# One block of filter rows first, the key weights in two halves, and a new written order

## The chip, the cores and the metric

The kernel runs on one core of a Trainium2 chip. The core has a matrix engine (TensorE, in the profile PE, with its weight loads as PEld), a vector engine (VectorE, DVE), an engine for functions (ScalarE, ACT), a general engine (GpSimd, POOL), and a queue engine that only issues transfers here (SyncE, SP). Sixteen DMA engines move the data. All times are device microseconds of one execution; the time of a kernel is the median of its runs.

## The reference

Two computations that share no data, both over 2048 positions and 576 channels in bf16, whose results stand beside each other in the output.

```python
# A: a long convolution with gates
k_shift = sum over t < 4 of shift(k, t) * shift_k[:, t]      # short filter over positions
kv = k_shift * v
y  = irfft(rfft(pad(kv)) * rfft(pad(ssm_k)))[:2048] + kv * ssm_D
a  = q * y

# B: linear attention, 32 heads of 18 channels
q, k, v = split(x @ wqkv)
phi(t) = (t + 1 if t > 0 else exp(t)) + 1e-6
kv  = phi(k).T @ v                 # per head, over all positions
z   = sum of phi(k) over positions
o   = (phi(q) @ kv) / (phi(q) . z + 1e-6)
b   = o @ wo

out = concat(a, b)
```

## The kernel before

The program builds a list of 838 operations (`P.op`, `load`), each with the buffers that it reads and writes. Their order, and for each the engine that runs it, is written out in the string `PLAN`: `P` is TensorE, `A` ScalarE, `D` VectorE, `G` POOL and `S` an issue on SP, followed by the operation's number. `PLACES` gives the address or PSUM bank of every buffer. `_issue` reads both; nothing is decided at run time. Every engine runs its operations strictly in that order and waits at each one until its operands are there and until the buffer that lay at the same address before has been used up. One more rule ties POOL to VectorE: a product or sum of POOL (marked `two`) waits for the last such product of VectorE that stands ahead of it in the order. SP issues its loads in order too, and no more than eight transfers are under way at a time.

Part A does the convolution as matrix products. The filter `ssm_k` comes in five blocks of up to 128 rows (`hs`); TensorE turns each (`htr`, L437), ScalarE or VectorE copies it to `hT` (`hev`), and POOL or VectorE adds `ssm_D` to its first tap (`hD`). For each of three groups of 192 channels follow a first transform (`s1h`, L468, eight products of four matmuls, each evicted to `Ch`), three transposes on VectorE (`trh`, L507), and a second small transform (`s2h`, L516, twelve groups of four matmuls on quarters of the array, evicted to `sph`). The data side is the same (`s1u`, `Cu`, `tru`, `s2u`, `spu`) after the short filter: VectorE multiplies the keys by the taps (`tap`, L402), the halves are summed (`tap+`) and multiplied by v (`tapv`), on VectorE or POOL; for two of the six pieces a DMA that POOL issues adds the first halves (`acc`, L408). Then two products of spectra (`p1`, `p2`, L236), an inverse transform in two stages (`i1`, L552, evicted to `V`; `i2`, L577, evicted to `yb`), the product with q (`yq`, or directly from PSUM as `i2q`) and the store (`yo`).

Part B turns the first 512 rows of x on TensorE (`xtr`, L323; its copies are `xev`, the copy of the last columns is `x4c`); the other rows come by a transposing DMA. For each of 16 blocks of 128 positions `kproj` makes the key product (`k`, L624: ten matmuls, two halves of 288 columns by five blocks of 128 rows of the weights `wk`), ScalarE its exponential (`kexp`) and VectorE phi (`kphi`). `qproj` (L645) does the same for q. `G` (L674) sums phi(k) with x over all positions; `kv` and `M` (L709, L771) fold the value and output weights into one matrix, `msev` (L802) scales its last rows; `den` and `rden` give 1 over the denominator, which goes to memory (`rw`) and comes back spread over rows (`rr`), and `pqn` multiplies phi(q) by it, on VectorE or POOL. `out` (L814) makes the output product, `oev` its copy and `oo` its store.

Ahead of everything TensorE runs nine matmuls on a constant (`fill`, L845). In the order before, SP issues first the two halves of x's first rows, the table with the identity (`idw`), the key weights (`wqktk`, then `wqkk` in one transfer, L355 and L357), `Drow`, then filter blocks 0 and 1 and one half of the transform's table, filter block 2, the other half, and the shift taps (`srow`). TensorE's order is: fill, the four steps of x, k1, k0, filter block 0, k2, filter block 1, then `s1h` of the first group.

Of the kernel before, what the change touches and what calls it, by code (L numbers as in the profile page):

```python
# [183 lines left out]
def kernel(  # L184
# [430 lines left out]
    def kproj(r):  # L615
# [2 lines left out]
        xT = xTg[r // 4]  # L618
        st = "k%d" % r

        def mm(e):
            for hh in range(2):
                for t in range(5):
                    nc.tensor.matmul(ps.t[:, hh, 0:HALF],  # L624
                                     lhsT=cols(xT.t[0:KT[t], t, :], r),
                                     rhs=wk.t[0:KT[t], t, HALF * hh:HALF * hh + HALF],
                                     start=(t == 0), stop=(t == 4))
        P.op("P", mm, rd=[wk] + ([xT] if r // 4 in XD else [(xT, (r % 4 // 2, t0)) for t0 in (0, 4)]), wr=[ps], name="k", mm=[(288, 128, 128)] * 10, st=st)
        P.op("A", lambda e: nc.scalar.activation(  # L629
            out=eb.t[:], in_=ps.t[:, :, 0:HALF], func=ACTF.Exp, bias=neg1.t[:]), rd=[ps, neg1], wr=[eb], name="kexp",  # L630
             n=576, st=st)
# [240 lines left out]
P98 S423 D35 S19 P95 P368 G0 D37 A15 A99 A369 S18 S41 P366 D100 G228 D367 P101 P375 A96 S472 D97 P372 A102 A377  # L872
A374 D376 P394 G4 D373 S59 D370 A395 P386 P392 D103 G10 G14 P384 P426 D387 A393 P424 G12 S56 G378 D385 A23 D427
P388 A425 P433 D379 G42 A434 P435 P382 S55 G428 D389 D436 P390 P380 P437 D391 A383 P443 D438 A381 P429 D405 P475
P441 A444 P431 D414 S24 S40 S58 P473 A430 A442 D396 P439 A432 A440 S60 P146 P417 A147 P415 S25 A474 G477 D476 D445
A418 P104 D148 A105 P143 S46 P401 P397 A416 P446 P448 S51 D106 P452 A144 P155 A449 A453 A398 D454 A402 P149 P152
A156 A150 D145 A447 S478 P408 D463 G47 D157 A153 P403 P399 P457 D151 A409 D400 S50 S45 P468 P170 A458 A404 P406
D469 P410 P461 D154 A462 D65 P459 P421 P161 A171 A411 P158 S48 A460 P412 S43 P466 P455 G52 D172 P419 D64 A407 A422
P164 D75 A456 P481 D74 D66 P470 A413 A467 P464 S230 P450 A420 P167 A165 G67 A451 A471 A162 D163 P479 A465 A480 A168
P197 D166 P200 A482 P191 A159 A192 D169 A201 D160 A198 D202 D193 P110 P185 D76 A111 G44 G483 D112 D199 P173 S594  # L880
A186 P134 P176 A174 G49 S61 D175 D187 A135 P122 A177 P179 G77 D178 D136 P107 S652 P119 A123 D124 A180 A108 P137 D78
D85 S229 A120 P188 D109 D181 A138 S595 D121 G68 S232 A189 P140 P128 S38 A141 D139 D190 P125 D84 A129 D142 P131 D130
P486 D86 P116 A126 A487 A132 A117 D127 P113 G87 S231 A114 S62 A39 S653 D133 D118 P194 P494 P182 D115 A183 P223 D88
A224 P484 A485 A195 D70 D79 A495 P226 A225 S17 P208 D69 D80 A227 S63 P236 D237 D238 P203 G71 D184 P239 D196 P243
P488 G81 D204 A209 A205 A210 P492 D240 D241 S552 D244 P498 A489 P206 D242 D245 A493 P490 A499 D72 D73 A491 P496
S553 S246 P218 A497 S247 A207 D219 P537 D220 A538 P531 S259 P529 A530 P221 P533 D82 S260 S258 P527 A532 A222 S254
D83 A534 P535 D89 A536 S261 P213 A528 P618 S265 P620 P608 P211 D90 A621 P610 A609 P606 D255 A212 D619 D266 A611
P614 D214 S269 G91 G270 P216 A607 D500 S252 P503 A215 P507 G262 A615 D518 P519 D509 P612 D217 A504 D508 P616 A520
D92 S263 S674 P541 P233 A613 P539 A617 A542 S271 A540 D93 P699 D235 P281 G272 D234 S267 P693 D700 P275 D694 A282
P273 P279 A276 A274 P277 D280 S248 A278 P691 A692 P685 P695 P283 D622 A696 S256 D686 P687 D284 S673 P629 P516 G253  # L890
A688 P627 P514 D517 P697 G264 D564 A630 P689 G268 A698 P332 A333 P347 A628 P355 A690 D664 G249 P357 P350 A356 A515
A351 P667 P669 D348 P671 A358 D585 S250 D701 A672 S631 P521 P512 G251 P505 P330 P352 A670 P327 P325 A513 A331 A668
D522 D353 A328 P665 D506 S573 P510 S574 D743 S22 P706 A326 P625 S329 P525 A666 P501 A511 P623 D643 A624 G257 P300
P345 S359 A707 P340 A626 P342 A341 A526 P302 P750 P704 P748 D502 P648 S354 G675 S632 A346 D301 P590 A343 D722 P650
G676 D705 D591 P362 S711 A649 D363 P360 P312 P567 A303 D651 A749 P565 A751 S731 P644 A361 S732 P523 D313 P646 A568
P744 S349 P708 A524 P315 D543 S753 D316 P310 P337 P317 D647 P569 A745 D311 S334 P586 D634 P725 A566 A645 S304 D655
P571 P723 A709 A338 P727 S364 A318 A728 P290 A726 S344 A587 P320 P683 A321 P307 A570 S319 A572 S314 D724 P729 P746
D291 A684 P702 P550 P548 D654 A703 P677 A747 P305 P660 P681 A306 A308 A661 D633 P641 S752 A682 P292 A551 P658 A293
A549 A659 P335 A642 D576 P679 A680 P297 A678 P635 D730 P546 P592 P544 D754 D755 D733 A336 S710 P588 D734 D713 A636
A593 A589 P756 P637 D712 A545 P295 A638 P639 A640 D298 P656 P737 A657 P739 A740 P662 A547 A738 A663 P741 P718 P720  # L900
P758 A721 P760 A759 P762 D757 P800 A801 A761 P735 D575 D555 S294 S94 P794 D296 A795 P796 D597 P802 D763 S339 A742
P577 D719 A803 A797 A736 D596 P806 S309 P716 P788 P714 A717 D554 P579 D804 A807 D798 P322 P808 A715 P824 P826 P790
S299 A323 D825 P832 A789 A791 P600 S324 P560 A809 A601 S799 A827 P581 A833 P812 P562 D792 P598 A599 D578 P814 D582
A561 D815 P830 A580 G810 G828 A563 S793 D813 P583 A584 D831 D816 S805 P558 P820 D821 G834 D559 P602 P556 S811 P818
P604 P285 D819 D603 A557 S829 S835 A605 D822 S817 D286 S823 P287 A288 S289 P784 P782 D785 A783 D786 P776 S787 A777
P778 A779 P772 D773 D780 S781 P764 P770 P766 D767 A771 D774 S775 A765 D768 S769
"""
PLACES = """
# [16 lines left out]
"""  # L925


# [28 lines left out]
```

## Time and profile before

| | us |
|---|---|
| median of 3 runs | 160.5 (160.44 to 160.75) |
| the profiled execution's own time | 161.04 |
| its span, first to last instruction | 159.2 |
| TensorE busy | 150.4 (94%) |
| VectorE busy | 143.3 (90%) |
| ScalarE busy | 122.7 (77%) |
| POOL busy | 63.2 (40%) |

The profile has one profiled execution. Its page gives busy time by engine, the span in 40 slices, the DMA queues, the chain of work that ended last, and the costliest groups of instructions. A group's line gives the source line, the engine, the operation, what it writes and reads, how often, its busy time, the mean duration of one in ns, the idle time of the engine ahead of it, and what ended that idle time. The view of windows gives the busy time by stage, the timeline the instructions in order of time, and the view of waits who waited for whom. A line L236, L231 or L229 is a helper's (products and sums, copies on VectorE, copies on ScalarE), so these are told apart by the names of what they write.

### The profile page before, as it was taken

What the parts mean: (1) busy time and instruction counts of PE and PEld (TensorE: products, weight loads), DVE (VectorE), ACT (ScalarE), POOL (GpSimd) and SP (SyncE); (2) the same over time, 40 slices, a digit from 0 to 9 for tenths busy, and PEclk for the clock granted to TensorE, in tenths of its full rate; (3) what the DMA queues carried; (4) which work ended last, traced back from release to release, by engine and by line L of the source; (5) the groups of instructions that cost most, each with busy time, mean ns of one, the idle gap of its engine ahead of it and who ended that gap; (6) DMA issues with size and microseconds to landing.
All of it is one profiled execution on the core that took longest, in us unless ns stands there. A gap on an engine that the chain in (4) does not pass through costs nothing.

```text
span 159.2 us, 4176 instructions
## 1 busy us (share of the span) xinstructions
PE 150.4 (94%) x1663; PEld 119.5 (75%) x1663; DVE 143.3 (90%) x183; ACT 122.7 (77%) x224; POOL 63.2 (40%) x51
## 2 busy tenths in 40 slices
PE   6897899999999999999999999999999999999970
PEld 2686785545677889787888878787777889999960
DVE  1537999999999999899899999999999999998981
ACT  3148799999996566561869599899989999896860
POOL 8901100110199170606920594996891000004400
PEclk9999999999999999999999999999999999999997
DMA  5999699999999128496925597891647449415575
GB/s 164 301 401 291 155 218 377 214 200 277 397 371 302 31 36 296 197 252 213 164 81 183 155 161 234 268 368 67 245 171 252 174 120 408 178 43 161 151 211 148
DMA packets 26317, 34.37 MB, mean 216 GB/s; under 512 B 15802, under 2 KB 20923, under 8 KB 25530
## 3 DMA queue, kind: packets, MB, share of 16 engines
q1 hardware_dynamic: 25754, 32.54, 65.8%
q0 software_dynamic: 544, 1.57, 5.6%
q8 instruction: 13, 0.21, 0.5%
q14 instruction: 6, 0.05, 0.1%
HBM read 20.86 MB, written 4.99 MB: 162 GB/s over the span
## 4 chain that ended last, share of the span: by engine, by line
PE 82%; DVE 5%; DMA 3%; ACT 3%; issue 2%; SPq 1%; DVEq 1%; ACTq 0%
PE ps_all L645 13%; PE ps_all L814 13%; PE ps_all L624 12%; PE ps_all L674 12%; PE ps_all L552 10%; PE ps_all L468 9%; PE ps_all L516 5%; PE ps_all L577 4%; DMA wk<-in_B_wqkv_dram 3%; DVE Cu L231 2%; PE ps_all L437 2%; SPq L222 1%; ACT sph L229 1%; PE ps_all L709 1%; DVE q L236 1%
## 5 line engine op out<-in xcount | busy, mean ns | idle before, releaser
L645 PE MATMUL ps_all<-xT,wq 128*126 128x512 bf16 (+1 forms) x100 | 24.0, 381 | 0.1
L814 PE MATMUL ps_all<-M,pqT 126*128 126x288 bf16 (+1 forms) x160 | 22.1, 287 | 0.0
L236 POOL TENSOR_TENSOR m<-m 128x1536 bf16<-128x1536 bf16 (+1 forms) x4 | 15.5, 3885 | 15.4 <-DVE m L236 15.4
L624 PE MATMUL ps_all<-wk,xT 128*128 128x288 bf16 x160 | 21.1, 286 | 0.5 <-DMA wk<-in_B_wqkv_dram 0.5
L402 DVE TENSOR_TENSOR m<-kh,Wj 128x3072 bf16<-128x3072 bf16 x12 | 20.5, 1752 | 0.1
L624 PEld LDWEIGHTS <-xT 128*128 128x128 bf16 x160 | 17.4, 109 | 3.6 <-issue 0.8
L814 PEld LDWEIGHTS <-pqT 126*128 126x128 bf16 (+1 forms) x160 | 16.8, 110 | 3.8 <-issue 2.0
L468 PEld LDWEIGHTS <-Gsb 128*128 128x128 bf16 x192 | 16.1, 98 | 4.2 <-issue 2.2
L645 PEld LDWEIGHTS <-wq 128*126 128x126 bf16 (+1 forms) x100 | 12.6, 131 | 7.9 <-issue 1.7
L552 PE MATMUL ps_all<-Esb,sph 128*128 128x128 bf16 x144 | 18.0, 219 | 0.0
L552 PE MATMUL ps_all<-Esb,X 128*128 128x128 bf16 x144 | 17.9, 219 | 0.0
L236 POOL TENSOR_TENSOR pqT<-pqT,rb 126x1024 bf16<-126x1024 bf16 (+1 forms) x8 | 16.8, 2138 | 2.5 <-DMA rb<-r_scr 2.1
L229 ACT ACTIVATE spu<-ps_all 128x512 bf16<-128x512 f32 x30 | 17.0, 636 | 0.6 <-PE ps_all L516 0.6
L229 ACT ACTIVATE Cu<-ps_all 128x768 bf16<-128x768 f32 x20 | 15.7, 853 | 2.0 <-PE ps_all L468 2.0
L229 ACT ACTIVATE V<-ps_all 128x512 bf16<-128x512 f32 x29 | 16.4, 661 | 1.2 <-PE ps_all L552 1.2
L674 PE MATMUL ps_all<-pk,x_sb 128*128 128x289 bf16 (+1 forms) x128 | 17.1, 287 | 0.0
L629 ACT ACTIVATE ek<-ps_all,neg 128x576 bf16<-128x576 f32 x16 | 11.7, 740 | 6.5 <-PE ps_all L624 6.4
L229 ACT ACTIVATE Ch<-ps_all 128x768 bf16<-128x768 f32 x18 | 14.2, 855 | 3.1 <-PE ps_all L468 3.1
L229 ACT ACTIVATE sph<-ps_all 128x512 bf16<-128x512 f32 x29 | 16.1, 625 | 0.3 <-PE ps_all L516 0.3
L648 ACT ACTIVATE eq<-ps_all,neg 126x512 bf16<-126x512 f32 (+1 forms) x20 | 13.7, 708 | 2.9 <-PE ps_all L645 2.6
L552 PEld LDWEIGHTS <-sph 128*128 128x128 bf16 x144 | 14.1, 98 | 0.7 <-issue 0.5
L674 PEld LDWEIGHTS <-x_sb 128*128 128x128 bf16 x128 | 12.3, 98 | 2.9
(97 smaller groups left out, 299.8 us busy)
## 6 DMA issues: line engine op xcount, KB each, us to landing
X<-sph SPq DMA_DIRECT2D x18, 256.0 KB, 4.7
v<-in_A_v_dram SPq DMA_DIRECT2D x2, 1152.0 KB
out_dram<-ob SPq DMA_DIRECT2D x16, 144.0 KB, 2.1
q<-in_A_q_dram SPq DMA_DIRECT2D x1, 2304.0 KB
out_dram<-q SPq DMA_DIRECT2D x12, 192.0 KB, 2.5
rb<-r_scr SPq DMA_DIRECT2D x8, 252.0 KB
x_sb<-in_B_x_dram SPq DMA_DIRECT2D x3, 576.0 KB
kh<-in_A_k_dram SPq DMA_DIRECT2D x1, 1584.0 KB
```

The lines of the kernel that those rows point to most:

```text
L229: nc.scalar.activation(out=o, in_=i, func=ACTF.Copy)
L236: return (nc.vector if e == "DVE" else nc.gpsimd).tensor_tensor(out=o, in0=a, in1=b, op=op)
L402: return nc.vector.tensor_tensor(out=m.t[:, i:i + 2], in0=i0, in1=i1, op=ALU.mult)
L468: nc.tensor.matmul(ps.t[:, bank, lo - 384 * bank:hi - 384 * bank], lhsT=Gsb.t[:, b, ri, :], rhs=src[:, lo - CC * j:hi - CC * j], start=Tru ...
L516: nc.tensor.matmul(ps.t[32 * j:32 * j + 32, 0, :], lhsT=W2()[32 * kh:32 * kh + 32, :], rhs=ct.t[32 * kh:32 * kh + 32, 8 * j:8 * j + 8], st ...
L552: nc.tensor.matmul(ps.t[:, 0, 128 * c:128 * c + 128], lhsT=src.t[:, 4 * hh + c, :], rhs=Esb.t[:, 32 + wi, :], start=(wi == 0), stop=(wi == 1))
L624: nc.tensor.matmul(ps.t[:, hh, 0:HALF], lhsT=cols(xT.t[0:KT[t], t, :], r), rhs=wk.t[0:KT[t], t, HALF * hh:HALF * hh + HALF], start=(t == 0 ...
L629: P.op("A", lambda e: nc.scalar.activation(out=eb.t[:], in_=ps.t[:, :, 0:HALF], func=ACTF.Exp, bias=neg1.t[:]), rd=[ps, neg1], wr=[eb], na ...
L645: nc.tensor.matmul(ps.t[0:hn, 0, :], lhsT=wq.t[0:KT[t], t, h0:h0 + hn], rhs=xT.t[0:KT[t], t, :], start=(t == 0), stop=(t == 4))
L648: P.op("A", lambda e: nc.scalar.activation(out=eb.t[0:hn], in_=ps.t[0:hn, 0, :], func=ACTF.Exp, bias=neg1.t[0:hn, :]), rd=[ps, neg1], wr=[eb],
L674: nc.tensor.matmul(ps.t[0:m, 0, 0:n], lhsT=x4[r // 4].t[:, r % 4, :] if t == 4 else x_sb[r // 4].t[:, r % 4, 128 * t:128 * t + 128], rhs=p ...
L814: nc.tensor.matmul(ps.t[:, 0, 0:HALF], lhsT=cols(pqT[r // 8].t[0:kn, c, 512 * (r // 4 % 2):512 * (r // 4 % 2) + 512], r), rhs=M.t[0:kn, c, ...
```

## The change

Three edits in the code. The key weights' four blocks of 128 rows come in two transfers of two blocks each (294,912 bytes) instead of one. For the first two blocks of positions the key product is split into two operations that add to the same PSUM sums: the first (`ka`) covers row blocks 0 and 1 for both halves of the columns and needs only the first transfer and the first four column blocks of x, the second covers row blocks 2, 3 and 4. The rest of `k` stays whole.

```diff
     def wload(which, key):
         c0 = which * D
         wx = wk if which else wq
-        load("wqk" + key, wx, lambda e: dma(e, wx.t[:, 0:4, :], ap(wqkv, c0, [[3 * D, 128], [3 * D * 128, 4], [1, D]])),
-             589824, 1152, wr=[(wx, "m")], engs=EARLY)
+        if which:
+            for u in range(2):
+                load("wqh" + key, wx, lambda e, u=u: dma(e, wx.t[:, 2 * u:2 * u + 2, :], ap(wqkv, c0 + 3 * D * 256 * u, [[3 * D, 128], [3 * D * 128, 2], [1, D]])),
+                     294912, 1152, wr=[(wx, u)], engs=EARLY)
+        else:
+            load("wqk" + key, wx, lambda e: dma(e, wx.t[:, 0:4, :], ap(wqkv, c0, [[3 * D, 128], [3 * D * 128, 4], [1, D]])),
+                 589824, 1152, wr=[(wx, "m")], engs=EARLY)
...
-        def mm(e):
-            for hh in range(2):
-                for t in range(5):
-                    nc.tensor.matmul(ps.t[:, hh, 0:HALF],
...
+        for u, ts in ((0, (0, 1)), (1, (2, 3, 4))) if r < 2 else ((2, (0, 1, 2, 3, 4)),):
+            def mm(e, ts=ts):
+                for hh in range(2):
+                    for t in ts:
+                        nc.tensor.matmul(ps.t[:, hh, 0:HALF],
+                                         lhsT=cols(xT.t[0:KT[t], t, :], r),
+                                         rhs=wk.t[0:KT[t], t, HALF * hh:HALF * hh + HALF],
+                                         start=(t == 0), stop=(t == 4))
+            rw = [wk] if u == 2 else [(wk, 0)] if u == 0 else [(wk, k) for k in (1, "o", "t")]
...
-G8 D836 P837 G5 G57 S26 G13 S28 G6 D27 S16 S54 S53 G3 P30 D29 D31 G11 G7 P36 P32 S21 S365 G1 G9 A33 S371 S20 G2 P34
...
+G13 S374 G0 A15 G8 G12 S26 S16 D839 P840 P30 G5 P378 G3 D380 S18 S28 A29 G1 G27 P34 A31 S53 A35 D379 S55 P32 G4
...
```

The program now has 841 operations, and both strings, `PLAN` and `PLACES`, are new from the first to the last entry (the numbers from 54 on are shifted by the three added operations). At the start SP's order is: filter block 1 (`hs`), the first half of x, the identity, the shift taps, the second half of x, the first half of the key weights, their last rows, `Drow`, the second half, filter block 0, then the transform's table and the further blocks as before. The store of the turned shift taps, which stood behind q's weights, follows them still, and its copy is VectorE's. TensorE's order is: fill, first step of x, one half of filter block 1, second and third step of x, the other half of block 1, the first steps of k0 and k1, the last step of x, the second steps of k0 and k1, k2, filter block 0, then `s1h`.

Behind that the kind of work in each stage is the same, in another sequence. VectorE has 176 operations instead of 183, ScalarE 230 instead of 223. From POOL to VectorE go three tap sums (one large, two small) and four `pqn`; from VectorE to POOL one small tap sum, one `tapv`, two `pqn`, two `yq`, and one `x4c`. One `hD` and the `p1` and `p2` of one group go each way. 81 evictions and small copies change between VectorE and ScalarE. The load of the second key tensor (`kh1`) now follows a `tap` of VectorE on the first one, whose place it takes, where it followed POOL's `tapv`. Ahead of the first `out` POOL's order is: `acc`, two `pqn`, a constant, one tap sum, one `pqn`. The last eight `i2` groups stand in the order 6, 7, 0, 1, 4, 3, 5, 2 (before: 7, 6, 4, 5, 3, 0, 2, 1).

More of the change, by code (lines that the diff above doesn't have):

```diff
@@ L619, in kproj @@
         st = "k%d" % r
-        def mm(e):
-            for hh in range(2):
-                for t in range(5):
[L624 to L628, printed above, removed]
+        for u, ts in ((0, (0, 1)), (1, (2, 3, 4))) if r < 2 else ((2, (0, 1, 2, 3, 4)),):
[7 more added lines that the diff above has]
+            rw = [wk] if u == 2 else [(wk, 0)] if u == 0 else [(wk, k) for k in (1, "o", "t")]
+            rx = [xT] if r // 4 in XD else [(xT, (r % 4 // 2, t0)) for t0 in ((0, 4), (0,), (0, 4))[2 if u == 2 else (1 if u == 0 else 0)]]
+            P.op("P", mm, rd=rw + rx, wr=[ps], name="k" if u else "ka", mm=[(288, 128, 128)] * (2 * len(ts)), st=st)
         P.op("A", lambda e: nc.scalar.activation(
@@ L876 @@
[L876 to L890, printed above, removed]
@@ new lines @@
+P432 D417 P438 P107 A435 P478 A433 S24 P436 D479 A439 A108 P440 P149 P404 A437 S41 A441 D109 P418 P402 P152 A405
+S59 S40 D466 D419 S61 P406 P400 D457 P424 D448 A403 A150 G42 A153 D154 P471 A472 P467 P173 A468 A407 A174 P146 P476
+A401 D175 P158 A425 D477 P455 P451 A147 A159 P415 D151 S60 P462 D416 A456 S25 D148 D160 A452 P155 S50 P473 P420 D66
+S51 A463 P411 S46 P460 P170 A421 A156 G480 A461 P164 A412 D157 S43 P413 P409 A165 S45 P453 A454 P449 A474 P161 D65
+D166 A410 D67 A450 D75 P167 A414 P469 P422 P464 P458 G52 A423 A470 A465 P200 A171 P197 S481 G44 A162 D76 A459 P203
@@ new lines @@
+D163 A201 D172 A168 P194 A195 A204 G47 P182 P482 D169 G68 A183 A483 P484 A198 D196 P179 A180 P176 P188 A485 S233
+A189 D205 D202 D486 D77 D181 P125 P140 D199 D190 D184 A177 S62 G69 P110 D178 S555 A126 D127 S17 S598 A141 D78 A111
+D142 P128 S576 S635 G79 S48 S634 S656 S38 P116 S556 D112 P143 P497 A129 D130 A117 D118 A144 P134 A498 A39 D85 G49
+S577 D145 A135 P137 P489 A490 S232 S597 D86 P113 S63 P119 A138 D136 D139 S655 P122 A114 D115 A120 A123 D121 D87
+P493 P131 D124 A494 A132 P185 D133 D88 P191 P226 P229 A227 A186 D89 A228 P216 D70 D187 D71 A192 D193 A230 P239 P499
@@ new lines @@
+D240 P495 D241 A217 A500 P242 D80 P246 P487 A496 P491 D243 A488 D244 P219 A492 D247 D248 S64 P501 D245 A218 G72
+P206 A220 P540 A502 S263 S262 P538 A207 P532 S234 D73 D74 A533 P214 S266 A539 P536 P221 D81 A208 D82 A537 D83 S249
+A541 D267 P530 S268 A531 P211 A222 A212 A215 D84 D91 P534 S274 A223 S235 S261 D90 A213 S270 A535 S272 P542 A543
+P209 S250 P696 P690 G92 D271 P544 A210 G269 A697 A691 P224 P611 A545 A225 P621 P615 P236 D503 A612 P613 A622 D512
+A616 D588 A614 D521 G273 S253 D238 D237 P698 P609 P623 D699 A610 P619 P282 D624 P280 S264 A620 P519 G275 D283 A281
@@ new lines @@
+P278 A520 D567 S251 P276 A279 P617 D277 P524 P284 S257 P506 A618 P593 P595 P589 A285 P570 A525 G93 D94 D594 D590
+G265 G258 S259 P286 D287 D546 P688 A596 A571 P526 A507 P504 A689 P568 P702 A527 P333 A569 A334 P694 A703 P335 D505
+D646 G254 A336 P692 D625 A695 P353 P355 S255 P330 D354 A693 P522 P510 D667 A356 A331 P528 P553 P632 A523 P628 P630
+A511 A629 D633 S676 P360 P363 A529 D631 S755 P348 S677 A554 A361 P340 P626 P672 A349 P551 G260 A673 D364 D256 A341
+D627 D252 P653 P670 S337 D552 P328 G636 S22 P700 A671 A701 P338 D329 D339 P293 D746 D704 A654 P574 P651 S357 A294
@@ new lines @@
+A575 S332 P674 P547 A548 G637 P508 P649 P513 A675 P295 P358 P288 D359 S342 A652 P345 P300 A296 P707 D650 A509 D346
+A514 A289 D301 P572 A573 P753 P751 P517 A708 P668 D754 P749 A518 A669 A750 S714 S362 P350 A351 D752 S352 P303 P313
+P320 P709 P549 D725 D314 P726 A304 P515 A516 P728 P711 A727 A321 P318 A319 S734 A729 S713 P343 D578 S756 S735 P298
+A550 D579 D678 A710 P365 P305 A344 P315 A306 D712 D557 P290 A299 P647 S307 A366 D679 A316 A291 P747 P591 S322 P705
+P730 P732 A648 A731 P640 A641 P642 A643 P586 A587 S367 P680 A748 P644 P684 D558 P308 A733 D657 D658 S347 S95 P559
```

30 lines of the change are left out of this document (10 added, 20 removed), and 32 rows, old and new, of the table PLACES.

## The prediction

> **What bounds the kernel now.** I read the busy shares first, then the busy time by stage, then the start and the end in order of time.
>
> ```profile
> PE 150.4 (94%) x1663; PEld 119.5 (75%) x1663; DVE 143.3 (90%) x183; ACT 122.7 (77%) x224; POOL 63.2 (40%) x51
> ```
>
> ```profile
> 0.00:5.28 5.28, 3.81 (x9) 1.31 (x10) 1.61 (x3) 1.28 (x1) 4.63 (x13) 1.00 0.58 162
> 5.28:14.50 9.22, 7.96 (x84) 7.02 (x83) 4.21 (x7) 4.58 (x8) 3.02 (x9) 1.00 1.07 371
> 14.50:24.60 10.10, 9.38 (x109) 7.84 (x108) 10.09 (x14) 8.57 (x12) 1.17 (x3) 1.00 0.85 206
> ...
> 40.20:66.90 26.70, 26.70 (x189) 21.22 (x188) 26.14 (x32) 18.68 (x29) 15.42 (x7) 1.00 0.69 237
> 66.90:97.90 31.00, 31.00 (x354) 25.74 (x353) 29.91 (x36) 21.98 (x36) 13.70 (x7) 1.00 0.66 174
> 97.90:104.30 6.40, 6.22 (x67) 4.79 (x65) 6.33 (x9) 5.94 (x11) 6.40 (x4) 1.00 0.86 255
> 104.30:152.20 47.90, 47.89 (x688) 41.37 (x687) 46.18 (x63) 44.00 (x96) 17.44 (x8) 1.00 0.55 192
> ```
>
> Columns: stretch, length, busy PE, PEld, DVE, ACT, POOL, clock, DMA share, GB/s. Two engines bind together. TensorE is full from 40.2 to 97.9 and from 104.3 to 152.2, and VectorE nearly full from 14.5 on. What both lack is the start: VectorE works 4.21 of the 9.22 us before 14.5. So the change is worth what it gives VectorE and TensorE there, less what the new order loses later. The start in order of time:
>
> ```profile
> 0.75 0.87 SPq L222 DMA_DIRECT2D x_sb<-in_B_x_dram  x2
> 1.47 4.02 PE L845 MATMUL ps_all<-cft 128*128 128x512 bf16 x9 [1.47 <-DVE cft L841]
> 3.71 1.12 DVE L231 COPY x<-x_sb 128x128 bf16<-128x128 bf16 x2 [2.29 <-DMA x_sb<-in_B_x_dram]
> 5.28 1.06 PE L323 MATMUL ps_all<-idw,x_sb 128*128 128x128 bf16 x8
> 6.56 0.85 PE L323 MATMUL ps_all<-idw,x_sb 128*128 128x128 bf16 x8
> 7.89 2.61 PE L624 MATMUL ps_all<-wk,xT 128*128 128x288 bf16 x20 [0.48 <-DMA wk<-in_B_wqkv_dram]
> 11.53 0.69 DVE L231 COPY hT<-ps_all 128x1024 bf16<-128x1024 bf16 x1 [0.60 <-PE ps_all L437]
> 12.56 1.16 PE L437 MATMUL ps_all<-idw,hs 128*128 128x128 bf16 x16
> 14.50 1.68 PE L468 MATMUL ps_all<-hT,Gsb 128*128 128x192 bf16 x15 [0.78 <-DVE hT L231]
> 15.64 0.96 DVE L231 CAST Ch<-ps_all 128x768 bf16<-128x768 f32 x1
> ```
>
> The fill (L845) ends at 5.28, TensorE then turns x (L323), waits for the key weights until 7.89, and only at 14.50 starts the filter transform (L468). VectorE evicts its first product at 15.64.
>
> **Step 1, the start.** 512 KB of filter rows go ahead of x. At 371 GB/s they take 1.4 us. The chain of waits has the weights' landing, and SP's waits and VectorE's are below it:
>
> ```profile
> 2.76 5.09 DMA wk<-in_B_wqkv_dram
> ...
> 27.39 0.78 PE ps_all L516 x20
> ```
>
> ```profile
> SPq L222 <- ACT srt L229: 3.7, 1, 3.7
> ```
>
> x landed by 3.71, so now by 5.1: still under the fill, nothing lost. The key weights landed at 2.76 + 5.09 = 7.85, so their second half lands at 9.26 and the first about 0.8 us (295 KB) before. Until then TensorE turns x (5.28 to 7.42 in the rows above), turns one block of filter rows (16 transposes, 1.0) and does the first steps of k0 and k1 (8 matmuls of 0.13, 1.0): 9.45, so the weights are hidden. Then 12 matmuls for the second steps (1.5), k2's ten (1.3) and the other block (1.0, its first half 0.5): 12.7 for that half, plus 0.69 of VectorE's copy, 13.4 for the first L468 product against 14.50. The second product, which VectorE evicts, is out at about 14.25 against 15.64: **1.4 us gained**. The matmul count is unchanged (the steps keep their sums open in PSUM); the added DMA costs SP one issue of about 0.5 us, ahead of nothing that TensorE waits for. The shift taps' small load moves up to fourth; the wait for its turned form (3.7 us of SP) goes, and SP has the loads behind it (transposes of x, first taps) out sooner, which VectorE did not wait for. POOL takes one copy of x columns (0.63 on VectorE), after memsets that take 4.63 us by 5.28; its result and the weights' constant rows are done before 9.26: nothing. Bounds: 2.0 if the halves also come faster, 0 if the filter block costs more queue time than TensorE can fill.
>
> One page speaks against this. The Trainium skill, "DMA: Bandwidth & Descriptors", section "Anatomy of one DMA", puts a fixed 2.0 us on every DMA (for POOL's path). If the two halves paid it one after the other, the second would land at about 11.3 and not 9.26, an estimate by that page, and the gain of step 1 would turn into a loss of 0.6. The two x loads above were issued back to back and TensorE read both without a pause, so the trace does not bear it out for SP's queue; a case of it stands under the second rival.
>
> **Step 2, VectorE up to msev.** Between the first eviction of L468 and the scaling that ends M (L802, "msev" here) I counted VectorE's instructions in both written orders and multiplied the differences by these means:
>
> ```profile
> L632 DVE SCALAR_TENSOR_TENSOR pk<-ek,ps_all 128x576 bf16<-128x576 bf16 x16 | 11.6, 751 | 2.4 <-ACT ek L629 2.3
> L507 DVE STREAM_TRANSPOSE ct<-Cu 128x1024 f32<-128x1024 f32 x9 | 10.8, 1223 | 0.1
> ...
> L231 DVE CAST Ch<-ps_all 128x768 bf16<-128x768 f32 x6 | 5.4, 949 | 0.0
> L236 DVE TENSOR_TENSOR m<-m 128x3072 bf16<-128x3072 bf16 x3 | 5.2, 1748 | 0.0
> L231 DVE CAST ob<-ps_all 128x288 bf16<-128x288 f32 x11 | 4.9, 446 | 0.2
> L236 DVE TENSOR_TENSOR v<-m,v 128x1536 bf16<-128x1536 bf16 x5 | 4.8, 956 | 0.6 <-POOL m L236 0.5
> L231 DVE CAST sph<-ps_all 128x512 bf16<-128x512 f32 x7 | 4.7, 676 | 0.1
> ```
>
> More: one large tap sum 1.75, one small 0.95, one transpose 1.22, two spectrum evictions 1.37, M 0.76, two small ones 0.7. Less: three evictions of L468 2.84, one product 0.96, one spectrum 0.68, G's five 1.5. Together +0.6 on 92.6 us of work. Against it stands the wait on POOL's sum (0.5 in the last row but one), which goes because VectorE does that sum itself. So msev moves from 102.67 (row below) by 1.4 - 0.6 + 0.5 to about 101.4, **1.3 us earlier**. ScalarE gets 2.8 us of evictions in all from the others; it has 8.0 us idle from 40.2 to 66.9 and 9.0 in the stretch behind, so I count nothing. A cover that is thinner: the second key tensor's load now waits for a VectorE tap, with six k evictions (0.75 each), two sums and a product behind it, 8.2 in all; 1.62 MB at 237 GB/s take 6.8. If that cover goes, VectorE waits for the difference.
>
> **Step 3, the first output product.** It needs msev and POOL's normalized q. The new order has there a chain of two engines: a DMA that adds two halves, POOL's tap sum, VectorE's product, then POOL's q (L236), then L814.
>
> ```profile
> 89.05 1.21 POOL L408 DMA_DIRECT2D m<-m  x1 [8.58 <-DVE m L402]
> ```
>
> ```profile
> L236 POOL TENSOR_TENSOR pqT<-pqT,rb 126x1024 bf16<-126x1024 bf16 x6 | 12.6, 2139 | 2.1 <-DMA rb<-r_scr 2.1
> L236 POOL TENSOR_TENSOR m<-m 128x1536 bf16<-128x1536 bf16 x3 | 9.3, 3095 | 15.4 <-DVE m L236 15.4
> ```
>
> ```profile
> m<-m POOLq DMA_DIRECT2D x2, 768.0 KB, 6.5
> ```
>
> ```profile
> 102.67 0.76 DVE L802 TENSOR_SCALAR M<-ps_all 32x576 bf16<-32x576 f32 x1
> ```
>
> ```profile
> 104.30 3.16 PE ps_all L814 x25
> ```
>
> VectorE's 92.6 us of durations took 87.8 (15.64 to 103.44), 0.948 each, since neighbours overlap. In the new order 79.0 of them stand up to its last tap before that DMA and 90.1 up to its product: 14.25 + 0.948 x 79.0 - 0.5 = 88.6 and 99.2. The adding DMA (6.5) and POOL's sum (3.1) make 98.2 of the first, 1.0 before VectorE is ready for the product; that (0.96) and q (2.14) make 102.3 for L814; msev ends at 102.2. TensorE's own work ahead of it is up to 0.5 more than before (three groups of L516 more), so 102.3 to 102.8. I take 102.7, nearest to a full TensorE, against 104.30: **1.6 us earlier**. Before, this chain had time to spare: POOL added its half at 89.05 and q was next needed at 104.30.
>
> **Step 4, TensorE behind it.** By the order one output product more stands behind that point (five of L814's matmuls, 0.63 by 25 in 3.16), and 38 of the small transforms' groups (L516) instead of 41, at 0.16 (0.78 for 5): 0.63 - 0.48 = **0.1 more**. TensorE is full there (47.89 of 47.90), so this counts whole. Bounds: 0.6 if the runs of L516 cost the same with fewer groups, and -0.2 if their small stalls go.
>
> **Step 5, the tail.**
>
> ```profile
> 151.34 2.80 PE L577 MATMUL ps_all<-V,Esb 128*128 128x192 bf16 x32
> ...
> 154.65 1.02 DVE L236 TENSOR_TENSOR q<-yb,q 128x768 bf16<-128x768 bf16 x2
> ```
>
> The last 8 groups of L577 are the same 2.80. VectorE ends 4.33 after their start. In the new order its last eviction waits for the last group, with two products behind others: 3.70 + 2 x 0.5 = 4.75: **0.4 later**. POOL's two products more end before.
>
> **Sum**: -1.6 + 0.1 + 0.4 = -1.1. The profiled execution took 161.04 (1.84 around its span of 159.2), so 159.9 for it. It lay 0.54 above the median of the runs, 160.5; against that median I put **159.4 us**.
>
> **Rivals.**
> *POOL's chain closes late (slower).* Place: step 3. The margin there is 1.0, and each us beyond goes to the end whole. If POOL still works on two q products (2 x 2.14) because their rows of 1/den land late, or the adding DMA takes 8 instead of 6.5, the sum comes 2 to 4 us late. It decides from 1.0 + 1.1 = 2.1 late on; at 3.1, the length of POOL's sum, 159.4 + 2.1 = 161.5. For it: POOL waited 2.1 for those rows before. Against: 1/den stands earlier in VectorE's new order, behind three taps instead of four.
> *The filter block delays everything (slower).* If the 512 KB cost 2.8 us ahead of x (the first stretch moved 162 GB/s and not 371), the weights' second half lands at 10.7, step 1 is gone (1.4), 160.8; if the fixed cost of two DMAs in a row comes true, 2.0 more than forecast, 161.4.
> *It cancels.* VectorE's gain of step 1 is lost in steps 3 and 5, 1.1 more than I count, for TensorE has no slack to make up: 160.5.
> *Nothing binds later.* VectorE also loses its idle 1.1 us between 66.9 and 97.9, and the tail costs nothing (0.4): 159.4 - 1.1 or so, 158.3.
>
> **Numbers.** Forecast 0.35, POOL's chain 0.20, filter block 0.15 (the page's rule 0.03 of it), cancels 0.15, nothing binds 0.15. Faster by over 0.2% (about what a measurement of this kernel can tell from no change, 0.3 us): 0.50; within: 0.15; slower: 0.35. The range takes in both ends: 158.2 to 161.6; the forecast's own is 158.9 to 160.1.
>
> **What would show it.** Right: first L468 at 13.4, VectorE's first eviction of it at 14.2, msev at 101.4, first L814 at 102.7, last L577 group at about 152.9. Wrong: a wait of L624 on the key weights past 9.5, POOL's sum ending after 99.5, VectorE waiting for the second key tensor, L814 waiting for POOL. The likeliest error is step 3, which I could not see in the profile of before.

## The result and the profile after

The change made the kernel slower: the median of 11 runs is 162.27 us, against 160.79 for the kernel before on the same chips, a ratio of 1.0078 with a 95% interval of 1.0056 to 1.010. The forecast was 159.4 and its range ended at 161.6. The profiled execution took 162.27, with a span of 160.5 us (159.2 before). Ratios here and below leave out executions over 1.5% longer than the fastest of the same kernel, while the medians are over all.

The busy times of TensorE and VectorE hardly differ from before (150.4 and 143.3), ScalarE has 3.2 us more and POOL 4.7 us less, so the loss does not show in the totals:

```profile
PE 150.5 (94%) x1663; PEld 118.8 (74%) x1663; DVE 141.9 (88%) x176; ACT 125.9 (78%) x231; POOL 58.5 (36%) x51
```

The timeline of VectorE (start, length, engine, line, operation, what it writes and reads, idle time before it and its releaser) shows the stretch up to the scaling that ends M, here L810:

```profile
15.11 1.84 DVE L231 CAST Ch<-ps_all 128x768 bf16<-128x768 f32 x2 [0.34 <-PE ps_all L473]
...
87.05 3.43 DVE L407 TENSOR_TENSOR m<-kh,Wj 128x3072 bf16<-128x3072 bf16 x2
...
100.01 0.72 DVE L231 CAST M<-ps_all 126x576 bf16<-126x576 f32 x1
101.66 0.96 DVE L236 TENSOR_TENSOR v<-m,v 128x1536 bf16<-128x1536 bf16 x1 [0.94 <-POOL m L236]
102.54 1.28 DVE L231 CAST spu<-ps_all 128x512 bf16<-128x512 f32 x2
103.85 0.76 DVE L810 TENSOR_SCALAR M<-ps_all 32x576 bf16<-32x576 f32 x1
```

VectorE's first eviction of the transform is 0.53 earlier than before (15.64), but msev is 1.18 later (102.67). Between them lies a wait of 0.94 on POOL's sum. The chain of work that ended last, which ran through TensorE there before, now goes through that sum; its columns are start, length and what ran:

```profile
91.03 7.37 DMA m<-m
...
98.53 3.10 POOL m L236
...
103.85 0.78 DVE M L810
...
105.15 0.62 PE ps_all L822 x5
```

The last line is the first output product: 105.15, before 104.30. As what released the adding DMA the profile names a transform product of TensorE (L473), ending at 90.91. But in all thirteen profiles that can be compared (without the first attempt at the start alone, below) this DMA starts 0.54 to 0.59 behind the end of VectorE's last tap, whatever L473 does, and in one of them (VectorE's q behind the last taps) it starts at 89.83, before that L473 ended at 90.17. So the tap is what it waits for.

Windows of both kernels divide the rest. First the kernel before, then the changed one; columns are stretch, length, busy PE, PEld, DVE, ACT and POOL with their instructions, clock, DMA share and GB/s:

```profile
15.64:103.44 87.80, 86.85 (x845) 66.31 (x844) 86.07 (x101) 69.25 (x113) 36.71 (x21) 1.00 0.78 218
104.30:154.14 49.84, 49.83 (x709) 43.08 (x707) 47.87 (x66) 45.55 (x100) 17.44 (x8) 1.00 0.57 195
154.14:159.20 5.06, 0.00 (x0) 0.00 (x0) 1.53 (x4) 0.58 (x2) 0.00 (x0) 0.81 0.58 155
```

```profile
15.11:104.62 89.51, 87.60 (x852) 66.24 (x850) 87.07 (x97) 72.05 (x120) 30.59 (x19) 1.00 0.84 222
105.15:155.20 50.05, 50.05 (x709) 43.37 (x706) 47.02 (x64) 45.42 (x100) 19.27 (x10) 1.00 0.57 187
155.20:160.50 5.30, 0.00 (x1) 0.00 (x0) 1.96 (x4) 0.49 (x1) 0.00 (x0) 0.95 0.56 150
```

From the first eviction to the end of msev VectorE needs 1.71 more: 1.00 more busy time (87.07 - 86.07) and 0.71 more idle time. Busy time counts a moment in which two instructions overlap once; the durations summed one by one rose by 0.7 (92.5 to 93.2), so some of the 1.00 is that neighbours overlapped less. From the first output product to TensorE's last matmul it is 0.21 more, from there to the end 0.24. So the 1.3 us of span are 0.85 that stand at the first output product and 0.45 behind it.

### The profile page after: what moved, and what is told of

Same layout as the page of the kernel before. It is cut to its first block, busy times and chain, and to the rows that moved or that the text cites. A ratio compares the mean times of both kernels' runs of the same rounds, so it can differ in the third digit from the quotient of the medians.

```text
span 160.5 us, 4160 instructions
## 1 busy us (share of the span) xinstructions
PE 150.5 (94%) x1663; PEld 118.8 (74%) x1663; DVE 141.9 (88%) x176; ACT 125.9 (78%) x231; POOL 58.5 (36%) x51
## 4 chain that ended last, share of the span: by engine, by line
PE 73%; DMA 8%; DVE 6%; issue 3%; ACT 3%; SPq 2%; POOL 2%; DVEq 0%; POOLq 0%
PE ps_all L822 13%; PE ps_all L653 13%; PE ps_all L682 11%; PE ps_all L630 11%; PE ps_all L557 10%; PE ps_all L473 6%; DMA m<-m 5%; PE ps_all L521 4%; PE ps_all L582 4%; DMA wk<-in_B_wqkv_dram 3%; SPq L222 2%; DVE ct L512 2%; POOL m L236 2%; ACT Ch L229 2%; PE ps_all L442 1%
## 5 line engine op out<-in xcount | busy, mean ns | idle before, releaser
L653 PE MATMUL ps_all<-xT,wq 128*126 128x512 bf16 (+1 forms) x100 | 23.4, 380 | 0.2
L229 ACT ACTIVATE Cu<-ps_all 128x768 bf16<-128x768 f32 x22 | 17.5, 850 | 2.4 <-DVE v L236 1.3
L473 PEld LDWEIGHTS <-Gsb 128*128 128x128 bf16 x192 | 16.1, 98 | 3.9 <-issue 3.1
L229 ACT ACTIVATE sph<-ps_all 128x512 bf16<-128x512 f32 x33 | 18.2, 609 | 0.5 <-PE ps_all L521 0.4
L557 PE MATMUL ps_all<-Esb,sph 128*128 128x128 bf16 x144 | 17.3, 219 | 0.0
L682 PE MATMUL ps_all<-pk,x_sb 128*128 128x288 bf16 (+1 forms) x128 | 17.1, 287 | 0.0
L229 ACT ACTIVATE Ch<-ps_all 128x768 bf16<-128x768 f32 x19 | 15.2, 863 | 1.7 <-PE ps_all L473 1.6
L229 ACT ACTIVATE V<-ps_all 128x512 bf16<-128x512 f32 x29 | 15.6, 634 | 0.7 <-PE ps_all L557 0.6
L229 ACT ACTIVATE spu<-ps_all 128x512 bf16<-128x512 f32 x26 | 14.9, 616 | 1.2 <-PE ps_all L521 0.7
L413 POOL DMA_DIRECT2D m<-m x2 | 2.5, 1272 | 33.5 <-PE ps_all L473 17.2
L640 DVE SCALAR_TENSOR_TENSOR pk<-ek,ps_all 128x576 bf16<-128x576 bf16 x16 | 11.6, 747 | 3.2 <-ACT ek L637 3.2
```

Of the source, the lines that this page charges most:

```text
L229: nc.scalar.activation(out=o, in_=i, func=ACTF.Copy)
L473: nc.tensor.matmul(ps.t[:, bank, lo - 384 * bank:hi - 384 * bank], lhsT=Gsb.t[:, b, ri, :], rhs=src[:, lo - CC * j:hi - CC * j], start=Tru ...
L557: nc.tensor.matmul(ps.t[:, 0, 128 * c:128 * c + 128], lhsT=src.t[:, 4 * hh + c, :], rhs=Esb.t[:, 32 + wi, :], start=(wi == 0), stop=(wi == 1))
L640: P.op("D", lambda e: nc.vector.scalar_tensor_tensor(out=pk[r // 4].t[:, r % 4, 0:D].rearrange("p (h c) -> p h c", h=2), in0=eb.t[:], scal ...
L653: nc.tensor.matmul(ps.t[0:hn, 0, :], lhsT=wq.t[0:KT[t], t, h0:h0 + hn], rhs=xT.t[0:KT[t], t, :], start=(t == 0), stop=(t == 4))
L682: nc.tensor.matmul(ps.t[0:m, 0, 0:n], lhsT=x4[r // 4].t[:, r % 4, :] if t == 4 else x_sb[r // 4].t[:, r % 4, 128 * t:128 * t + 128], rhs=p ...
```

## The experiments

My theory after the result: the start is a small gain, and the loss is the late end of the chain of taps, adding DMA, POOL's sum and VectorE's product. Rivals: the start itself is the loss (512 KB ahead of everything), or VectorE's added work holds TensorE whatever the chain does. All ratios are to the kernel before, run in turn with it on the same chip.

**The split of the key weights alone.** Before's order; the two halves are issued one behind the other (the entries' numbers shift by the added operations).

```diff
-S54 S53 ... P98 ... P95
+S55 S53 S54 ... P100 P101 ... P96 P97
```

> Before's written order and places, with one thing of the change alone: the key weights come in two transfers issued one behind the other, and k0 and k1 are each two operations one behind the other on TensorE. Theory: nothing uses the first half earlier and one more issue costs SP about 0.5 us, so TensorE's first key product starts at 7.9 to 8.4 (before 7.89) and the time stays within 0.3 us of before, ratio 0.998 to 1.003. Rival (a transfer has a fixed cost that is paid twice): the key products start at 9 or later, ratio 1.006 or more.

Measured: 160.82 against 160.85, ratio 0.9996 (0.9975 to 1.0016). The key products start even earlier than before (7.89), since the first half serves the first steps:

```profile
7.33 2.87 PE L630 MATMUL ps_all<-wk,xT 128*128 128x288 bf16 x20 [0.60 <-DMA wk<-in_B_wqkv_dram]
```

The second half did not pay a fixed cost of its own. The prediction set against this a rule of the Trainium skill, "DMA: Bandwidth & Descriptors", section "Anatomy of one DMA"; by it, as an estimate, the second half would have held these products up to about 9.9, and all twenty were done by 10.20. The page gives that cost for POOL's path; on SP's queue here the halves overlap, for they landed at 7.29 and 8.04, 0.75 apart.

**The start alone, first attempt.** The change's order up to the transposes ahead of the first transform (64 entries), before's order behind it, before's addresses.

```diff
-G8 D836 P837 G5 G57 S26 ...
+G13 S374 G0 A15 G8 G12 S26 S16 D839 P840 P30 ... P369 P395 A370 D106 ...
```

> The change's order up to the last filter block's transposes ahead of the first transform (64 entries), and before's order behind it, with before's places but for five early buffers. Theory (the start by itself is a small gain, the loss lies in the later order): the first transform product at 14.2 and VectorE's first eviction of it about 0.5 us earlier than before's 15.64, msev and the first output product earlier by up to 0.5, time 0.2 to 0.5 us below before, ratio 0.997 to 0.999. Rival (the start is the loss, through the 512 KB ahead of everything): ratio 1.003 or more. Rival (a later wait swallows it): 1.000.

Measured: 169.03, ratio 1.0509. This says nothing on the start. The address of the shift taps lay within the constant that the fill reads, so SP stood still before that load, with x's second half and the key weights behind it:

```profile
1.67 0.43 SPq L222 DMA_DIRECT2D idw<-tab_i  x1
7.02 0.59 SPq L222 DMA_DIRECT2D srow<-in_A_shift_k_dram  x1
7.65 0.58 SPq L222 DMA_DIRECT2D x_sb<-in_B_x_dram  x1
```

An order alone is not the schedule; the addresses add waits to it.

**The start alone, at the changed kernel's early addresses.** The same order; the addresses of the early buffers (shift taps, filter rows, key products, their exponentials) are the changed kernel's, or free ones.

```diff
-srow 16544  cft 16512
+srow 27360  cft 21216
```

> The same order as in the run of the start alone, with the early buffers at the changed kernel's addresses, so that SP no longer stops for 4.9 us on an address that the fill still reads. Theory (the start by itself is a small gain): first transform product at 14.2 to 14.4, VectorE's first eviction of it at about 15.1 (15.64 before), everything behind it earlier by the same amount, ratio 0.996 to 0.998. Rival (the start is a loss): 1.003 or more. Rival (swallowed by a wait behind it): 1.000.

Measured: 160.35, ratio 0.9969 (0.9946 to 0.9992): the start is a gain of 0.5 us. Its first transform product is at 14.01 and VectorE's first eviction at 15.20; from 18 us on VectorE runs 0.36 to 0.51 ahead of before at every instruction that both have, to the end. TensorE waited for the second half of the key weights until 9.78, though, and not 9.26. That leads to the next run.

**Two small loads behind the key weights** (in the changed kernel).

```diff
-... S18 S28 ... S53 ... S55 ... S21 D382 S54 ...
+... S28 ... S53 ... S55 ... S54 S18 S21 D382 ...
```

> The changed kernel with the two small loads (shift taps, ssm_D) issued behind the second half of the key weights and not ahead of it. Theory 1 (SP's issues set the landing): the second half is issued 1.0 us earlier and lands at about 9.0 instead of 9.97, TensorE's wait of 0.88 on it goes, the first transform product starts at 13.4 to 13.6 instead of 14.25; ratio to before 1.003 to 1.005. Theory 2 (the bytes ahead of it set the landing): it lands at 9.8 to 10.0 as before, and the ratio stays 1.008.

Measured: 161.85, ratio 1.0062 (1.0039 to 1.0085), above the 1.003 to 1.005 expected; first transform product at 13.40, just as forecast, with no wait on the weights. The last key-weight packets landed at 8.24 here, 8.36 and 8.15 in two further profiles with the small loads behind, and between 8.60 and 9.89 in the seven with them ahead (9.60 in the changed kernel's profile).

That the issues set the landing is not shown by this. A load is done when sixteen parts of it have each reported. Thirteen of the second half's sixteen had by 8.10 to 8.56 with the small loads behind and by 8.31 to 8.72 with them ahead, although it was issued at 3.73 here and at 4.92 in the changed kernel. Only the last few parts differ: in the changed kernel fifteen had reported by 8.97 and the sixteenth came at 9.97, and in four of the seven profiles with the small loads ahead TensorE waited 0.23 at most. One late part also comes with the small loads behind: at 9.87 in the profile of a later run with that order (before's order with the improved start, first version), an execution longer than that kernel's others. So it stays open whether the order of the issues or the chance of an execution makes the last part late. The times don't tell either, since the interval overlaps the changed kernel's.

Of the 0.85 that VectorE was ahead of the changed kernel at its first eviction, only 0.25 was left 4 us later:

```profile
14.26 1.82 DVE L231 CAST Ch<-ps_all 128x768 bf16<-128x768 f32 x2 [0.34 <-PE ps_all L473]
16.14 0.69 DVE L231 COPY hT<-ps_all 128x1024 bf16<-128x1024 bf16 x1
17.44 2.69 DVE L231 CAST Ch<-ps_all 128x768 bf16<-128x768 f32 x3 [0.62 <-PE ps_all L473]
```

TensorE was there waiting for the second half of the transform's table, 0.48.

**The table's half with less beside it.** The same, with the transposing load of x ahead of the fourth filter block, which so starts later.

```diff
-S19 ... S475 ... S57 S56 ... S41
+S19 S41 ... S475 ... S57 S56
```

> The kernel with the small loads last, and the transposing load of x moved ahead of the fourth filter block, so that this block and q's weights are issued some us later and share less with the second half of the transform's table, on which TensorE waited 0.48 and VectorE 0.62 at 16.8. Theory (every us that VectorE gains before about 18 stays to the end): that wait goes, VectorE's first transpose starts at 19.4 instead of 20.05, and 0.5 to 0.6 go from the end: ratio to before 1.002 to 1.003. Rival (the table is late whatever shares with it): 1.006.

Measured: 161.49, ratio 1.0049 (1.0024 to 1.0073), above the 1.002 to 1.003 expected. That wait is gone from the trace, and VectorE's gain stays. The step from one run to the next (0.0016, then 0.0013) is less than its interval, so I rely on the traces for its size.

**POOL's last sum cut to one eighth** (in the changed kernel). Seven eighths of the columns of one tap sum are left out.

```diff
-P.op("DG", lambda e: tt(e, m.t[:, 0], m.t[:, 0], m.t[:, 1], ALU.add),
+na = 1 if (cc, bh) == (2, 1) else 8
+P.op("DG", lambda e: tt(e, m.t[:, 0, 0:na], m.t[:, 0, 0:na], m.t[:, 1, 0:na], ALU.add),
```

> The changed kernel with POOL's last tap sum cut from eight blocks of columns to one (1536 elements to 192), order and places untouched. Seven eighths of that sum are left out, so that part of the convolution's input lacks half of its taps. Theory (the late end of this sum is what moves the first output product): the sum ends by 99.0 instead of 101.65, VectorE's product starts at 100.7 without a wait, POOL's q ends at 103.9 (104.81), msev at 103.7 (104.61), ScalarE's eviction behind the product starts by 101.8 (102.70), the first output product at 104.2 (105.15), and the end 0.9 earlier: ratio 1.0078 - 0.0056 = 1.002. Rival (VectorE's work holds TensorE as long): 1.007 to 1.008.

Measured: 160.72, ratio 1.0005 (0.998 to 1.003): 1.2 us less than the changed kernel, and as fast as before. The 1.2 is the difference of two ratios, each with its interval, so it is uncertain by some 0.5 us. POOL's and VectorE's timelines, and from the chain that ended last the first output product:

```profile
97.85 0.55 POOL L236 TENSOR_TENSOR m<-m 128x192 bf16<-128x192 bf16 x1 [1.32 <-DMA m<-m]
```

```profile
100.05 0.94 DVE L236 TENSOR_TENSOR v<-m,v 128x1536 bf16<-128x1536 bf16 x1
100.91 1.28 DVE L231 CAST spu<-ps_all 128x512 bf16<-128x512 f32 x2
102.22 0.76 DVE L811 TENSOR_SCALAR M<-ps_all 32x576 bf16<-32x576 f32 x1
```

```profile
103.52 0.62 PE ps_all L823 x5
```

The product no longer waits, and the first output product is at 103.52 (expected 104.2, changed kernel 105.15). Against the changed kernel VectorE is 0.60 ahead up to M's eviction (97.59 against 98.19; this execution's weights landed earlier) and 1.63 from msev on, and stays so to the last instruction. So 1.03 of the profile comes with the sum's late end, and the rival that VectorE's work holds TensorE anyway falls as the main cause; the remainder is dealt with below. This run only left work out, so it is a measurement and no remedy.

Four runs then moved single entries around that place, to see whether the wait can be filled and what stands behind the product.

**Evictions and POOL's q both ahead of the product.**

```diff
-G93 D94 D594 D590 G265 G258
+G93 G265 D594 D590 D94 G258
```

> The changed kernel with three entries moved: the two evictions of the data's second transform that stood behind VectorE's product with v go ahead of it, and POOL's q that stood behind that product goes ahead of it too, right behind POOL's sum. Theory (the chain of POOL's sum holds up VectorE by 0.94 and, through the product, POOL's q): the evictions fill the wait, msev ends near 103.9 (104.61), q ends near 103.8 (104.81), the first output product starts at 104.3 to 104.5 (105.15), ratio to before 1.0078 - 0.005 = 1.003. Rival (TensorE is bound elsewhere and the wait costs nothing at the end): 1.008.

Measured: 164.2, ratio 1.0186 (1.0139 to 1.0232), slower by 1.7 us than the changed kernel: my expectation was wrong. POOL, VectorE, ScalarE and TensorE around 102:

```profile
101.46 2.11 POOL L236 TENSOR_TENSOR pqT<-pqT,rb 126x1024 bf16<-126x1024 bf16 x1
```

```profile
102.32 2.06 DVE L236 TENSOR_TENSOR v<-m,v 128x1536 bf16<-128x1536 bf16 x1
```

```profile
104.47 0.60 ACT L229 ACTIVATE spu<-ps_all 128x512 bf16<-128x512 f32 x1 [2.42 <-issue]
```

```profile
105.12 0.61 PE L521 MATMUL ps_all<-ct,idw 32*32 32x512 bf16 x8 [1.94 <-ACT spu L229]
```

The product beside POOL's q took 2.06 and not 0.96. ScalarE's next eviction writes to the place of the taps (`spu` at 189920 reaches into `m` at 192640), so it stood until the product ended at 104.38, and TensorE 1.94 behind it. I had counted VectorE's wait and POOL's q, not this third one that hangs on the product.

**Only the evictions ahead.**

```diff
-G93 D94 D594 D590 G265
+G93 D594 D590 D94 G265
```

> The changed kernel with only the two evictions moved ahead of VectorE's product; POOL's q stays behind it. Theory (ScalarE's evictions into the place of the summed taps, and POOL's q, stand behind the product, so the product is what must come early): the product starts near 102.3 and lasts 0.96, POOL's q ends near 105.4, TensorE stalls 0.5 us longer on ScalarE's eviction, ratio 1.010 to 1.012. Rival (only VectorE's own wait counts, and the evictions fill it): 1.003.

Measured: 163.52, ratio 1.0111 (1.0059 to 1.0162), as expected. POOL's sum ended at 100.92 there (97.82 + 3.10), and the product, behind the evictions, began only at 101.75; it kept its 0.95, but ScalarE's eviction and POOL's q came later with it. That filling VectorE's wait is worse is read from the trace, where the product began 0.83 after the sum's end: the time can't tell, since its interval overlaps the changed kernel's, and the profiled execution took 162.25 although its sum ended 0.7 earlier than the changed kernel's. The product is what must come early.

**Only POOL's q ahead.**

```diff
-G93 D94 D594 D590 G265
+G93 G265 D94 D594 D590
```

> The changed kernel with only POOL's q moved, ahead of VectorE's product and so beside it. Theory (products of VectorE and POOL slow each other, 2.06 against 0.96 where both moves were made): the product takes about 2.0 and ends near 103.7 (102.62), msev ends near 105.7, POOL's q near 103.8 (104.81); first output product 105.9 to 106.3, ratio 1.012 to 1.016. Rival (POOL's q is what the first output product waits for): 1.004 to 1.006.

Measured: 164.94, ratio 1.0162 (1.0099 to 1.0225). The size is as expected, but its profiled execution (162.54) was the fastest of its six, and there the product came first, at 101.85 with 0.96, and POOL's q behind it took 2.90 (median 2.14). That the other five lost to the opposite order is argued, not shown.

**VectorE's q behind the last taps**, to start the chain earlier.

```diff
-D267 ... D84 D91 ... D90 ... S270
+... D84 D91 ... D90 D267 ... S270
```

> The changed kernel with one entry moved: VectorE's first q (0.68 us), which stood ahead of the last two taps, goes behind them. Nothing is left out. Theory (POOL's sum ends late because its chain of taps, adding DMA and sum starts late): the adding DMA starts at 90.3 instead of 91.03, the sum ends at 100.9 instead of 101.65, VectorE waits 0.1 to 0.3 instead of 0.94, msev and the first output product come 0.6 to 0.7 earlier; ratio to before 1.0078 - 0.0042, about 1.0035. Rival (the rows for the later q are loaded into the place of this q's rows, so SP and POOL's own q come later and push the sum back): 1.008 or more.

Measured: 171.81, ratio 1.0683. The adding DMA did start earlier, at 89.83. But the rows for the next q are loaded into the place of this one's, and now they were issued after it:

```profile
93.45 0.69 DVE L236 TENSOR_TENSOR pqT<-pqT,rb 126x1024 bf16<-126x1024 bf16 x1 [3.57 <-DMA rb<-r_scr]
```

SP, POOL's q and its sum slid with them, and TensorE stood for 8.19 us from 95.43. The rival was right, and far larger than I had it.

**A version faster than both.** Before's order behind the change's start, with the small loads behind the key weights (diffs as above); then the same with the identity's load first of all (`S16` ahead of `S374`).

> Before's order behind the change's start, as in the run before last, with the two small loads behind the key weights. Theory: first transform product at 13.4, VectorE's first eviction at 14.3, of which what is not lost on the table's second half stays to the end: 0.5 to 1.2 us below before, ratio 0.993 to 0.997. Rival (swallowed): 0.999 to 1.001.

> The improved start on before's order, with the identity's load issued first of all, ahead of the filter block. Theory: TensorE's wait on the identity (0.1 to 1.45 in the profiles with this start) goes, the filter block and x land 0.2 later, VectorE's first eviction at 14.0 to 14.3; ratio 0.992 to 0.995. Rival (x's landing is the bound anyway): 0.995, as without it.

Measured: 160.12, ratio 0.9948 (0.9924 to 0.9972), and 160.23, ratio 0.9945 (0.9923 to 0.9967). The first's profiled execution took 162.62 (its eleven others 159.37 to 160.75), so I read the trace of the second. There TensorE does not wait for the identity, the last half of the key products starts at 9.17 with no wait and the first transform product at 13.40. But the order of the two first loads made no difference to the time: x's landing bounds there, TensorE waits for it until 5.80. Both beat the kernel before by 0.8 to 0.9 us.

## Why the prediction was wrong, step by step

The forecast took the right place for the risk, the end of POOL's chain, and put it at 0.20 and 161.5; that rival came true in place and size (160.5 x 1.0078 = 161.75). Of the causes that it named, only a longer DMA came, at 7.37 and not 8; no q product held POOL, and the tap that came 1.9 late it did not name. So that its 161.5 is so near is in part luck. What failed is the margin of 1.0 that step 3 gave it.

- **Step 1, the start: right in sign, too large.** Forecast 1.4; measured 0.53 at VectorE's first eviction in the profile, and 0.5 us as time for the start alone. What failed is the landing of the second half, forecast for 9.26: TensorE waited for it until 10.02. Shift taps and ssm_D stood ahead of it on SP's queue, and the prediction put the issues ahead of it at nothing; but that they made it late is open (the run with the small loads behind). The 0.53 itself is one draw: in six profiles with the very same order of issues VectorE's first eviction came between 14.17 and 15.37, in four of them at 14.17 to 14.59, near the forecast's 14.25. The forecast of the bytes (512 KB in 1.4 us) held for x's first half, which landed by 5.2 where 5.1 was forecast.
- **Step 2, VectorE up to msev: wrong.** The added work, counted as the forecast did by summed durations, was 0.7, near its 0.6; as busy time it was 1.00. In place of the wait on POOL's sum that was to go (0.5) another came: 0.94 on POOL's last sum. Without that one the idle time fell by 0.23. That gives -0.53 + 1.00 + 0.71 = +1.18 instead of -1.3. The thinner cover of the second key tensor held: VectorE never waited for it.
- **Step 3, the first output product: the deciding failure.** VectorE's last tap ended at 90.48 (87.05 + 3.43) and not 88.6. Of these 1.9 the start is 0.86. Another 0.5 is the wait that I subtracted: it did go (0.46 at 66.43 before), but 0.59 on ScalarE's exponentials and 0.22 on the first adding DMA came, so that VectorE's idle time up to the tap was 1.36, before 1.35. The last 0.5 is overlap: the count of durations was right (79.1, forecast 79.0), but 74.00 of busy time came of them, where before 71.47 came of 76.8. From there to POOL's sum I put the DMA's 6.5; it took 8.05, since POOL began the DMA 0.55 after the tap and it then took 7.37. That DMA took 7.28 to 7.37 in all seven profiles in which SP issues six row loads beside it, 6.40 to 6.43 in the six with before's order, where one is issued during it, and 8.11 in the run with VectorE's q behind the taps, where two are issued at its start. What lengthens it was not found. With the late tap and the longer DMA the sum ended at 101.6, 3.4 later than forecast, while VectorE was ready 1.5 later than forecast: the margin of 1.0 became a wait of 0.94. Such a gap was to be seen before: that DMA began at 89.05, and VectorE's last tap had ended at 88.47. The output product came at 105.15 instead of 102.7.
- **What hangs on the product** was counted as two things, msev and POOL's q. ScalarE's evictions into the taps' place are a third, which the buffers' addresses show and the order doesn't.
- **Steps 4 and 5: right in size, step 5 in part by luck.** Forecast 0.1 and 0.4, measured 0.21 and 0.24. In step 5 VectorE ended 4.97 behind the start of the last groups (forecast 4.75, though its sum gives 4.70; before 4.33), which is 0.64 more, but what follows VectorE's end was 0.37 shorter (3.13 against 3.50), and the forecast had no term for that.
- **The rival of the filter block** falls with the start alone at 0.9969, a fixed cost paid twice with the split alone at 0.9996. The rival's 2.8 us for 512 KB should have been 3.2 at its 162 GB/s, so 161.2 and not 160.8. **Nothing binds later** falls as well.

In times: start -0.5, POOL's chain +1.2, and the rest, by difference from +1.25 in all, about +0.55: what VectorE's added work leaves at the first output product, and the tail. The first two are uncertain by about 0.4 to 0.5 us each, so the third is a remainder and no measurement.

## What to carry to other kernels

A gain at the start of a kernel whose vector engine is nearly full is kept to the end only if no later chain closes late, so follow each chain that crosses two engines and a DMA from its first instruction to its last, with the gaps between them (tap to DMA 0.55, DMA 7.37, sum 3.10), and compare its end with the engine that reads it. Before moving an entry, look up what else lives at its buffers' addresses: three of the moves here lost about 2 to 10 us to a write that waited for the place, none of which the written order shows. And when a load is split to use its first half early, find out for the second half too when its last part lands, and in several executions: in the changed kernel's profile the last of its sixteen parts came 1.0 us behind the one before it.

## What the runs showed of the hardware

**TensorE's clock fell after a stall of 1.94 us.** In the run with evictions and q both moved, TensorE stood from 103.18 to 105.12, and the granted clock (the third column from the end) dropped behind it:

```profile
106.00:108.00 2.00, 2.00 (x15) 1.56 (x13) 1.97 (x3) 2.00 (x5) 2.00 (x2) 0.58 0.12 45
108.00:110.00 2.00, 2.00 (x12) 1.55 (x11) 1.46 (x2) 1.39 (x4) 2.00 (x2) 0.56 0.03 8
110.00:112.00 2.00, 2.00 (x37) 1.50 (x39) 1.56 (x2) 1.65 (x5) 0.83 (x1) 1.00 0.00 0
```

During the stall of 8.19 in the run with VectorE's q behind the taps it fell to 0.57 (99 to 101) and 0.50, and it stayed at 0.50 until 112, 8.4 us after TensorE had resumed at 103.62:

```profile
101.00:103.60 2.60, 0.00 (x0) 0.00 (x0) 2.50 (x5) 0.00 (x0) 0.73 (x2) 0.50 0.67 243
...
110.00:112.00 2.00, 2.00 (x27) 1.03 (x8) 1.29 (x2) 2.00 (x5) 2.00 (x2) 0.50 0.33 131
```

So a stall costs more than its length. After a stall of 1.50 in the run with only q moved the clock stayed at 1.00. The Trainium skill, "TensorE: Matmul & The Clock Gate", section "Why this matters for your kernels", asks for no gaps above some 3 us; here 1.94 sufficed, with shorter gaps of 0.45 and 0.22 in the 8 us ahead of it.

**Products of VectorE and POOL take turns.** 2.06 instead of 0.96 for VectorE's where POOL's q had begun 0.86 before it, 2.90 instead of 2.14 for POOL's where VectorE's had begun 0.03 before it. In both cases the later one ended about its own length after the earlier one's end (103.57 + 0.96 = 104.5 against 104.38; 102.81 + 2.14 = 104.95 against 104.78). The Trainium skill, "SBUF — State Buffer", section "SBUF: two separate sides", says that when a product of VectorE has two inputs in SBUF and POOL's operation reads SBUF too, the port pair that they share goes to whichever starts first for the whole instruction; the trace agrees.

**The start varies from one execution to the next.** With the very same order of issues, the first transform product came at 13.32 to 14.52 in six profiles. In the two latest (14.25 and 14.52) TensorE had waited 0.88 and 1.50 for the key weights; in the other four (13.32 to 13.73) 0.23 at most.
